# A new order of steps, more dummy products and items of 608 slots in a fused attention and two-layer expert kernel

## The chip, the cores and the metric

The kernel runs on one NeuronCore of one Trainium2 chip. The metric is the device time of one execution in microseconds (us). Five instruction streams work side by side: TensorE (PE, matrix products and transposes), VectorE (DVE), ScalarE (ACT), GpSimd (POOL) and SyncE (SP, which here only issues DMAs). Each runs its own list strictly in order and waits on the others by semaphores.

## The reference

```python
def _attn_ref(q, k, v, omega):              # (4, 8, 576, 64), 128 random features
    phi(x): h = x*scale @ omega.T - |x*scale|^2/2;  exp(h - max(h)) / sqrt(m)
    kv = phi(k).T @ v;  z = sum(phi(k))     # per batch and head
    return (phi(q) @ kv) / (phi(q) @ z + 1e-6)

def _moe_ref(x, w_in, w_out, g_ln):         # x: 2304 tokens x 512
    h = x @ w_in                            # 512 -> 1024
    solu = h * softmax(h)
    ln = (solu - mean) / sqrt(var + 1e-6) * g_ln
    return ln @ w_out                       # 1024 -> 512

def _moe2_ref(x, w_gate, w_output_gate, w1, w2):   # 8 experts, 512 -> 1024 -> 512
    e_idx = argmax(x @ w_gate);  gate_w = softmax(x @ w_gate)[e_idx]
    eom = sigmoid(x @ w_output_gate)
    for e in range(8):
        out[e_idx == e] = gate_w * eom[:, e] * (relu(x @ w1[e]) @ w2[e])
```

All is float32. With the inputs as drawn (seed 0) the eight experts get 561, 576, 0, 0, 0, 591, 576 and 0 of the 2304 tokens; four of them work.

## The kernel before

**The front.** The 2304 tokens are 18 tiles of 128. Every tile passes a chain of small steps, and each step is a function with a short name and the tile's number. `kp2` is the feature product of tile 2's keys on TensorE, `kx2` its maxima on VectorE, `ke2` its exponentials on ScalarE, `kv2` and `kw2` its part of the sums over the keys; `qp`, `qx`, `qe` are the same for queries, `qta`/`qtb` transposes of them, `qca`/`qcb` their copies, `na`/`nb`/`nc` the products with the sums, `ya`/`yb`/`yc` the divisions on VectorE, `xt` the transpose of the tile of x, `xh` and `xl` its upper and lower half. All large float32 products are made as three products of such halves (`mm3`): upper by upper, upper by lower, lower by upper. `ha`/`hb` are the two halves of h, `hxa`/`hxb`, `he`, `ma`, `mz`, `mb`, `mc`, `md`, `me` the softmax and the normalisation, `ta`/`tb` transposes, `u`/`l` the halves of the second product, `ua`, `ub`, `la` what takes them out of PSUM, `lo` the store. `ra` to `rh` work out the place of each token in its expert's list for six sets of tiles, and `zl` to `wc` load and split the first expert's weights and gather its first 256 tokens.

The weights of the first layer come as 16 chunks of eight-byte words. VectorE turns a chunk into float32 in five passes (`db`, `dc`, `dd`, `de`, `df`, L263 to L284), with one addition on POOL (`dp`) and a last pass for the lower half (`dl`). `ga` to `gd` fold the gate into the second weight.

`ORDER` is a table, written out by hand or by a planner, of all these steps. The helper `in_order` chains every instruction to the one before it on its engine, so that each engine runs its instructions in just this order. `LOADS` is the order of the loads on the SP queue; `pump` issues the next load as soon as the ring of buffers for its kind has one that the list has already used up. Work buffers are few: `big` has four PSUM half-banks (a feature product takes two), `sm` two.

**Dummy products.** A step `wuN` (`warm`) issues N products of a constant tile of ones with itself, 128x128, into columns of the PSUM bank of the key sums that nobody reads. A float32 product shows as two records in the trace.

**The experts.** Tokens are handled in items of `CAP` slots of one expert; `NSURE` is the number of items that is always run, `ceil(2304 / CAP)`, here 4, and more follow only if the experts' counts need more. `up` makes the hidden layer of an item for its slots (8 blocks of 128 features, 12 products each) in two runs of columns, `down` the output in blocks of 128 slots (`NBLK` = 5 blocks, 24 products each), scatters each block by an indirect DMA, and between the blocks the next item's tokens are transposed (`xpose`). The first item is split: its first 256 slots (`CA * P`) are run first, while the places of the last tiles are still being worked out (`rest`).

```python
    in_order(begin, 0)
    for what in ORDER:
        ...
        name = what.rstrip("0123456789")
        in_order(steps[name], int(what[len(name):]))
```

Of the kernel before, what the change touches and what calls it, by code (L numbers as in the profile page):

```python
# [67 lines left out]
ORDER = """
    da0 wu9 kp2 kx2 ke2 db0 da4 dc0 dd0 wu10 kp0 de0 df0 dp0 dh0 kx0 db4 dc4 dd4 de4 df4 wu4 kp1 ke0 dl0 dp4 kx1 da3
    wu10 kp3 db3 ke1 kv0 dc3 dd3 de3 df3 da6 wu2 kv1 kx3 dp3 dh4 da2 db6 dc6 dl4 dd6 de6 wu6 kp4 db2 dc2 dh3 dd2 da5  # L70
    de2 df2 ke3 df6 dl3 dp6 kx4 dh6 da1 wu12 kv2 dp2 dl6 kv3 ke4 db5 dh2 dc5 dd5 qp1 de5 df5 kv4 da8 dl2 qx1 dp5 da9
# [2 lines left out]
    qtb0 qcb1 kp7 da11 nb1 kx7 yb1 wu3 xt1 dp7 qcb0 dp9 ke7 dl8 qp2 db11 dc11 dd11 kv6 xh1 da10 dg9 qx2 de11 kp8 dh9
    df11 db10 qe2 na0 dc10 dl9 kv7 xl1 ya0 kx8 ga1 qta2 gb1 nb0 qca2 dp11 dg11 dd10 de10 ke8 df10 gc1 yb0 dp10 na2 gd1
    dg10 ya2 xt0 da12 ga3 dh11 qtb2 db12 dc12 kv8 gb3 dd12 qcb2 dl11 dh10 de12 dh7 nb2 xh0 df12 dl7 dp12 ga2 vc1 xl0
    qp4 gb2 yb2 da13 ha0 qx4 dg12 dh12 db13 qe4 dc13 dd13 de13 xt2 hb0 df13 dp13 xh2 hxa0 da15 xl2 dg13 dh13 qp3 hxb0
    gc2 he0 qx3 gc3 gd2 ma0 qe3 gd3 ga5 mz0 db15 ga4 mb0 gb5 dc15 qta3 gb4 qtb3 gc5 qca3 dd15 qcb3 ta0 mc0 gd5 de15
    na3 dl10 ca0 nb3 ya3 da14 sa0 tb0 kp9 db14 cb0 yb3 dc14 ha1 sb0 dd14 kx9 de14 ke9 hb1 df14 hxa1 dp14 df15 dg14
    qta4 hxb1 qtb4 dp15 dh14 gc4 he1 dl14 kv9 dg15 gd4 qca4 ma1 qcb4 na4 dh15 mz1 xt3 dl15 mb1 ga7 ya4 xh3 ga6 gb7  # L80
    kp10 xl3 gb6 mc1 ta1 kx10 gc6 ca1 ha2 md1 dl13 ke10 sa1 gd6 dl12 qp5 hxa2 hb2 qx5 qe5 nb4 hxb2 nc4 yb4 he2 kv10
    md0 yc4 me0 ma2 xt4 gc7 xh4 mz2 qta5 xl4 mb2 qtb5 qca5 gd7 tb1 qcb5 qp6 cb1 mc2 na5 sb1 qx6 u0 md2 qe6 ha4 ub0
    qta6 hxa4 qtb6 qca6 ya5 hb4 qcb6 na6 hxb4 ua0 nb6 he4 ya6 u1 ma4 mz4 mb4 ta2 kp12 ca2 yb6 mc4 sa2 me1 ta4 l0 ub1
    kx12 ua1 ca4 sa4 ke12 tb4 l1 la0 cb4 lo0 sb4 tb2 kp11 cb2 sb2 nb5 kx11 yb5 me2 ha3 ke11 md4 hb3 hxa3 la1 lo1 xt5
    hxb3 u2 xh5 he3 xl5 ma3 qp7 ua2 mz3 l2 ub2 mb3 qx7 mc3 qe7 md3 ta3 tb3 xt6 kv11 ca3 cb3 sa3 xh6 kp13 sb3 la2 xl6
    qta7 lo2 kx13 qtb7 qca7 me3 kv12 qcb7 ke13 na7 zc0 nb7 ya7 kv13 yb7 qp8 vc2 ha5 qx8 qe8 hb5 hxa5 u3 hxb5 he5 ma5
    ha6 mz5 ub3 ra0 mb5 hb6 hxa6 ta5 hxb6 tb5 ca5 u4 he6 me4 sa5 cb5 ua3 sb5 l4 ma6 ua4 ub4 qta8 la4 qtb8 qca8 lo4
    kp14 qcb8 na8 kx14 nb8 ya8 ke14 qp9 yb8 xt8 qx9 xt7 kw13 xh8 xh7 xl8 xl7 ha8 hb8 hxa8 u5 hxb8 qe9 mz6 he8 mb6 mc5
    ma8 ta6 tb6 ca6 l3 mz8 mc6 md5 sa6 mb8 cb6 md6 me5 sb6 me6 ub5 qta9 la3 ta8 tb8 ca8 lo3 kv14 qca9 qp10 ua5 na9 sa8
    mc8 qx10 cb8 qtb9 l5 md8 ya9 qe10 sb8 rc0 qcb9 kp15 la5 kp16 kx15 u6 kx16 ke15 ke16 l6 ub6 ua6 qp11 la6 kp17 qx11  # L90
    kv15 kx17 qe11 nb9 kv16 yb9 ke17 xt9 qta10 qta11 xh9 qca10 xl9 me8 lo5 qtb10 ha7 rd0 qcb10 qca11 na10 hxa7 nb10
    ya10 hb7 yb10 xt10 hxb7 qtb11 xh10 na11 he7 xl10 ha9 ya11 qcb11 ma7 mz7 hb9 mb7 hxa9 mc7 md7 me7 lo6 ta7 hxb9 tb7
    ca7 kv17 cb7 sa7 he9 sb7 nb11 ma9 u7 vc3 yb11 mz9 qp12 ua7 ub7 ra1 rc1 qp13 qx12 l7 qx13 qe12 rb0 qe13 ha10 re0
    rf0 rg1 la7 rg0 lo7 qta13 qtb13 hxa10 qca13 mb9 hb10 qcb13 mc9 md9 me9 u8 hxb10 he10 ma10 rb1 ua8 na13 ub8 ta9
    ya13 nb13 ca9 mz10 qta12 yb13 mb10 xt11 qca12 tb9 sa9 xh11 l8 mc10 xl11 cb9 md10 sb9 ha11 la8 hb11 hxa11 u9 hxb11
    he11 ma11 ta10 ua9 tb10 ca10 na12 ub9 mz11 cb10 mb11 rd1 rh0 sb10 rh1 qtb12 ya12 nc13 qcb12 rg3 ta11 nb12 yc13
    ca11 sa10 xt13 yb12 qp15 xh13 sa11 xt12 xl13 qp16 qx15 xh12 xl12 lo8 u10 qe15 qx16 qe16 l10 tb11 qta15 qtb15 me10
    re1 ub10 mc11 ua10 md11 la10 qca15 l9 qcb15 cb11 sb11 qp14 la9 lo9 u11 qx14 me11 lo10 qe14 na15 ub11 ra2 ua11
# [5 lines left out]
    tb14 ca13 sa14 cb14 ha16 sa13 ub12 xt17 tb13 xh17 rg11 sb14 rg10 rh10 rh11 cb13 hxa16 xl17 la12 sb13 hb16 lo12
    md14 me14 ha17 hxb16 he16 ma16 u13 mz16 mb16 mc16 hb17 ub13 hxa17 ua13 u14 hxb17 he17 md16 me16 ma17 l14 ua14 ub14
    mz17 ra3 mb17 rb3 mc17 ta17 rc3 tb17 ta15 rd3 re3 ca17 rf3 cb17 rg13 zl0 wa0 l13 rg12 mc15 sa17 rg14 rh12 la14
    rh13 ta16 la13 md15 md17 lo14 sb17 me17 wa1 rh14 lo13 zb0 ca16 tb16 u17 cb16 sa16 wa2 sb16 ca15 zg0 sa15 u16 wa3
    ub17 wb1 wc0 ua17 tb15 ua16 ub16 zt0 cb15 l17 me15 zh0 sb15 zs0 zg1 u15 wb2 wc3 la17 lo17 l15 ub15 ra4 ua15 rc4
# [1040 lines left out]
```

## Time and profile before

| | us |
|---|---|
| median of 3 timed runs | 661.83 (661.37 to 673.13) |
| the profiled execution | 665.99 |
| its span, first to last instruction | 664.3 |
| TensorE busy in the span | 639.2 (96%) |
| VectorE busy | 358.8 (54%) |
| ScalarE busy | 296.7 (45%) |
| POOL busy | 163.8 (25%) |
| mean granted TensorE clock | 0.983 of full |

Read it thus. TensorE is the engine that is nearly always busy, but three things are in its 96% that are not the reference's work: the dummy products, products at half the clock, and the modelled ends of pipelined products. What counts is therefore the spacing of its instructions, from the start of one to the start of the next, and not the length of a record. The front ends, and the experts begin, at about 417 us of the span.

### The profile page before, as it was taken

The numbers are of one execution on the slowest core, as the hardware profiler recorded it, in microseconds if no ns is written. First come the engines' busy times: TensorE is split into PE (matmuls) and PEld (weight loads), VectorE is DVE, ScalarE is ACT, GpSimd is POOL, SyncE is SP. The second block draws the span as 40 slices with busy tenths as digits, with TensorE's granted clock in tenths as the row PEclk, the third lists the DMA queues.
The fourth block names the chain that finished last, engine by engine and source line by source line (L and its number), as shares of the span: only waits on it lengthen the run. The fifth ranks groups of instructions, "written<-read, shape, count | busy, mean of one in ns | idle before, by whom it ended". The sixth has DMA issues, their size and how long they took to land. (4 is left out here: it accounts for less than half of the span.)

```text
span 664.3 us, 11388 instructions
## 1 busy us (share of the span) xinstructions
PE 639.2 (96%) x4434; PEld 582.0 (88%) x4434; DVE 358.8 (54%) x1010; ACT 296.7 (45%) x719; POOL 163.8 (25%) x133
## 2 busy tenths in 40 slices
...
GB/s 293 303 156 96 143 2 64 1 67 79 65 33 1 159 33 2 33 17 28 6 1 18 143 32 51 156 86 313 181 129 78 165 114 127 17 47 9 1 33 42
DMA packets 35199, 55.22 MB, mean 83 GB/s; under 512 B 2624, under 2 KB 21440, under 8 KB 35137
## 3 DMA queue, kind: packets, MB, share of 16 engines
...
q14 instruction: 26, 0.20, 0.1%
...
## 5 line engine op out<-in xcount | busy, mean ns | idle before, releaser
L155 PE MATMUL x<-w2h,lth 128*128 128x256 f32 (+1 forms) x288 | 83.8, 291 | 1.4 <-DVE xr L485 1.3
L155 PE MATMUL x<-w2l,lth 128*128 128x256 f32 (+1 forms) x288 | 81.9, 284 | 0.0
L155 PE MATMUL x<-w2h,ltl 128*128 128x256 f32 (+1 forms) x288 | 81.9, 284 | 0.0
L930 DVE SCALAR_TENSOR_TENSOR htl<-hp,hth 128x320 fp32r<-128x320 f32 (+2 forms) x64 | 31.4, 491 | 87.3 <-ACT hth L929 76.8
L558 POOL TENSOR_SCALAR s<-s,st 128x1024 f32<-128x1024 f32 x18 | 23.3, 1294 | 201.9 <-DVE st L554 93.4
L155 PE MATMUL hp<-xth,w1h 128*128 128x320 f32 (+1 forms) x224 | 70.3, 314 | 0.9 <-DVE htl L930 0.9
L155 PE MATMUL hp<-xtl,w1h 128*128 128x320 f32 (+1 forms) x224 | 70.2, 313 | 0.0
L155 PE MATMUL hp<-xth,w1l 128*128 128x320 f32 (+1 forms) x224 | 70.1, 313 | 0.0
L155 PE MATMUL yp<-w2h,hth 128*128 128x512 f32 x160 | 64.2, 401 | 0.0
L155 PE MATMUL yp<-w2l,hth 128*128 128x512 f32 x160 | 63.2, 395 | 0.0
L155 PE MATMUL yp<-w2h,htl 128*128 128x512 f32 x160 | 63.0, 393 | 0.0
L929 ACT ACTIVATE hth<-hp 128x320 fp32r<-128x320 f32 (+2 forms) x64 | 28.1, 439 | 74.4 <-PE hp L155 74.2
L155 PE MATMUL h<-w1h,xth 128*128 128x512 f32 x144 | 58.9, 409 | 0.0
L155 PE MATMUL h<-w1l,xth 128*128 128x512 f32 x144 | 56.9, 395 | 0.0
L155 PE MATMUL h<-w1h,xtl 128*128 128x512 f32 x144 | 56.9, 395 | 0.0
L155 PEld LDWEIGHTS x<-w2h,lth 128*128 128x128 f32 x288 | 54.1, 188 | 2.9 <-issue 1.5
L155 PEld LDWEIGHTS x<-w2l,lth 128*128 128x128 f32 x288 | 54.2, 188 | 0.3
L155 PEld LDWEIGHTS x<-w2h,ltl 128*128 128x128 f32 x288 | 54.3, 189 | 0.0
L525 DVE TENSOR_REDUCE st<-h 128x1 f32<-128x512 f32 x36 | 24.8, 689 | 45.2 <-PE h L155 45.2
L143 DVE TENSOR_TENSOR xtl<-xT,xth 128x512 fp32r<-128x512 f32 x36 | 24.7, 687 | 40.7 <-ACT xth L835 38.2
L372 ACT ACTIVATE qe<-qps,qmx 128x128 f32<-128x128 f32 x144 | 39.0, 392 | 17.1 <-DVE qmx L365 17.1
L951 ACT ACTIVATE y<-yp,scs 128x512 f32<-128x512 f32 x20 | 13.8, 690 | 69.3 <-PE yp L155 61.0
...
## 6 DMA issues: line engine op xcount, KB each, us to landing
...
```

What stands on the lines that cost most here:

```text
L143: return eng.tensor_tensor(out=out_, in0=a, in1=hi.bitcast(F32), op=ALU.subtract)
L155: return in_turn(nc.tensor.matmul(ps, **kw))
L372: nc.scalar.activation(out=e3[:, 2 * c + j, :], in_=pss[j][:, c, :], func=AF.Exp, bias=nmx[:, j, c:c + 1])
L525: nc.vector.tensor_reduce(out=st[:, n:n + 1], in_=of[f"h{n}", t], axis=AX.X, op=ALU.max, negate=True)
L558: nc.gpsimd.tensor_scalar(out=s, in0=s, scalar1=st[:, 10:11], scalar2=st[:, 11:12], op0=ALU.mult, op1=ALU.add)
L929: act = nc.scalar.activation(out=hi, in_=ps[:, 0:n], func=AF.Relu)
L930: dve = nc.vector.scalar_tensor_tensor(out=lo, in0=ps[:, 0:n], scalar=0.0, in1=hi.bitcast(F32), op0=ALU.max, op1=ALU.subtract)
L951: nc.scalar.activation(out=y, in_=ps, func=AF.Copy, scale=scs[:, col:col + 1])
```

## The change

Items have 608 slots instead of 640. The number of blocks stays 5, and the last block of an item has 96 slots: its gather, its transposes, its products in `down` and its scatter work on 96 rows. In `up` the two runs of columns of an item are 304 and 304 instead of 320 and 320, and in the first item 256 and 352 instead of 256 and 384. `NSURE` stays 4 (2304 / 608 = 3.8) and `NITEM` 11. Since a place within an expert's list no longer splits into item and slot by powers of two, `re` has three more small VectorE operations for each of the six sets: place is counted in units of `SHORT` = 32, and one is added for each item that lies before it. `LOADS` and `ORDER` are new tables with the same steps, but for the dummies: 14 groups with 83 products instead of 10 groups with 64. `warm` may now open the sums of a later batch, too.

```diff
-CAP = 640
-NBLK = CAP // P
+CAP = 608
+NBLK = -(-CAP // P)
+SHORT = NBLK * P - CAP
+def slots(j):
+    return min(P, CAP - j * P)
 LOADS = [(x[0], int(x[1:])) for x in """
-    k2 w0 w3 k0 w4 k1 w2 k3 v1 v0 v3 w6 c1 k5 w8 k4 w5 w9 c0 v2 w1 k6 v4 q1 q0 v5 k8 w7 k7 q4 k10 w11 q2 v7 v6 k11 v8
+    k0 w1 k3 w2 v0 k2 k4 k1 w3 w5 v1 w0 c1 q1 c0 k5 w9 w7 k6 w6 k7 w8 q2 q0 v2 w4 v3 v4 v6 q4 v7 k8 v5 k9 v8 w13 w11
 ...
 ORDER = """
-    da0 wu9 kp2 kx2 ke2 db0 da4 dc0 dd0 wu10 kp0 de0 df0 dp0 dh0 kx0 db4 dc4 dd4 de4 df4 wu4 kp1 ke0 dl0 dp4 kx1 da3
+    da1 wu9 kp0 wu4 kp3 kx0 db1 dc1 dd1 kx3 de1 ke0 df1 dp1 da2 wu8 kp2 ke3 kx2 wu5 kp1 dh1 db2 dc2 ke2 dl1 dd2 de2
 ...
-            if 0 not in kv_ps:
-                open_sums(0)
+            if not kv_ps:
+                open_sums(len(opened))
 ...
-            V.tensor_scalar(out=place, in0=place, scalar1=-1.0, scalar2=None, op0=ALU.add)
+            V.tensor_scalar(out=place, in0=place, scalar1=-1.0, scalar2=1.0 / SHORT, op0=ALU.add, op1=ALU.mult)
+            for k in range(1, NSURE):
+                V.scalar_tensor_tensor(out=place, in0=place, scalar=float(k * (CAP // SHORT + 1) - 1), in1=place,
+                                       op0=ALU.is_ge, op1=ALU.add)
             pli = r("pli", [P, n], I32)
-            V.tensor_copy(out=pli, in_=place)
+            V.tensor_scalar(out=pli, in0=place, scalar1=float(SHORT), scalar2=None, op0=ALU.mult)
 ...
         def xpose(x, xt, blocks, name):
             for j in blocks:
+                k = slots(j)
...
-                    transpose(ps[:, c, :], x[:, j, c * P:(c + 1) * P])
+                    transpose(ps[:, c, :], x[0:k, j, c * P:(c + 1) * P])
 ...
     def down(i, ht, blocks, between={}):
         for j in blocks:
+            k = slots(j)
...
-                mm3(ps, ht[0][:, f, j * P:(j + 1) * P], ht[1][:, f, j * P:(j + 1) * P],
+                mm3(ps, ht[0][:, f, j * P:j * P + k], ht[1][:, f, j * P:j * P + k],
```

Two places show how the new table moves instructions. The first is on TensorE, where the key sums of the second batch are opened (`kv1`, its dummies are the products with `ones`; `woT` are `ga`, `qT` are `qta` and `qtb`, `wog` is `gc`, `num` is `na`). Before:

```order
L155 MATMUL kv1_0_496<-ones_62 128x128 x5
L158 MATMUL woT0_567<-ident_61,f8_437 128x128 x4
L158 MATMUL qT1_0_574<-ident_61,qe1_457 128x128 x4
L155 MATMUL kv1_0_496<-v5_398,ke5_519 128x65 x4
L155 MATMUL kv1_1_497<-v5_398,ke5_519 128x65 x4
L155 MATMUL wog0_608<-glw_96,ft0_589 128x16 x4
L155 MATMUL num1_0_614<-kv_98,qt1_591 128x65 x4
L158 MATMUL qT0_0_624<-ident_61,qe0_506 128x128 x4
```

The same place on TensorE now:

```order
L162 MATMUL kv1_0_583<-ones_62 128x128 x12
L162 MATMUL kv1_0_583<-v5_593,ke5_413 128x65 x4
L162 MATMUL kv1_1_584<-v5_593,ke5_413 128x65 x4
L162 MATMUL kv1_0_583<-v6_442,ke6_564 128x65 x4
L162 MATMUL kv1_1_584<-v6_442,ke6_564 128x65 x4
L162 MATMUL kv1_0_583<-ones_62 128x128 x2
L166 MATMUL woT1_631<-ident_61,f9_542 128x128 x4
L166 MATMUL qT0_0_637<-ident_61,qe0_574 128x128 x4
L166 MATMUL qT1_0_647<-ident_61,qe1_504 128x128 x4
L162 MATMUL wog1_652<-glw_96,ft1_644 128x16 x4
```

Twelve dummies and two tiles' sums now stand in a row ahead of the first transposes, where five dummies and one tile's sums stood between them.

The second is on VectorE at the end of the front, before the experts' first products, which read `xtel` and `w1l`. `ea`/`er` are `rg`, `tsc` and `gw` are the last operations of `rf`, `lg` is `ub`, `ltl` is `sa`/`sb`. Before:

```order
L757 TENSOR_TENSOR gw_15_4794<-gw_15_4794,eo_15_4754 128x2
L759 CAST gwh_15_4801<-gw_15_4794 128x2
L760 COPY tsc_99<-gwh_15_4801 128x2
L761 TENSOR_TENSOR tsc_99<-gw_15_4794,gwh_15_4801 128x2
L768 TENSOR_SCALAR ea15_4805<-nums_97,flo_15_4790 128x128
L770 SCALAR_TENSOR_TENSOR er15_4807<-nums_97,col_15_4788,tsc_99 128x480
L143 TENSOR_TENSOR xtel_4483<-xTe_1_4811,xteh_4482 128x4x128
L768 TENSOR_SCALAR ea16_4855<-nums_97,flo_15_4790 128x128
L770 SCALAR_TENSOR_TENSOR er16_4857<-nums_97,col_15_4788,tsc_99 128x480
L973 COPY got_4874<-tab_2941 128x480
```

The same place on VectorE now:

```order
L781 TENSOR_SCALAR ea15_4800<-nums_97,flo_15_4716 128x128
L783 SCALAR_TENSOR_TENSOR er15_4802<-nums_97,col_15_4714,tsc_99 128x480
L150 TENSOR_TENSOR xtel_4547<-xTe_0_4769,xteh_4546 128x4x128
L150 TENSOR_TENSOR ltl17_4659<-lT17_1_4720,lth17_4658 128x512
L150 TENSOR_TENSOR w1l_72<-raw1_4543,w1h_71 128x1024
L150 TENSOR_TENSOR xtel_4547<-xTe_1_4808,xteh_4546 128x4x128
L781 TENSOR_SCALAR ea16_4822<-nums_97,flo_15_4716 128x128
L783 SCALAR_TENSOR_TENSOR er16_4824<-nums_97,col_15_4714,tsc_99 128x480
L150 TENSOR_TENSOR w1l_72<-raw1_4543,w1h_71 128x1024
L629 TENSOR_SCALAR lg_64<-x2_17_1_4827,st17_4468 128x16
```

The small operations of the last sets (`ra5`, `rf`) that stood between the two parts of `xtel` are now ahead of both or behind both, and both `w1l` passes stand in this place, one on each side of the second part. On TensorE the second transpose of the gathered tokens (`zt1`) had one product step behind it before the experts' first product, `l16`; now it has two, `u17` and `l17`.

## Rows read from the trace of the kernel before

**Rows 1.** The page: TensorE's share, and its granted clock in 40 slices.

```profile
PE 639.2 (96%) x4434; PEld 582.0 (88%) x4434; DVE 358.8 (54%) x1010; ACT 296.7 (45%) x719; POOL 163.8 (25%) x133
...

```

**Rows 2.** Windows: stretch, then each engine's busy us, clock, DMA share, GB/s.

```profile
20.00:40.00 20.00, 18.18 (x173) 17.37 (x172) 18.97 (x36) 13.89 (x44) 7.82 (x6) 0.93 0.76 230
...
60.00:80.00 20.00, 18.28 (x150) 16.41 (x149) 17.93 (x41) 12.30 (x32) 10.70 (x7) 1.00 0.39 123
80.00:100.00 20.00, 19.15 (x100) 17.48 (x100) 14.49 (x38) 11.23 (x30) 4.22 (x4) 0.66 0.14 51
```

**Rows 3.** Timeline of VectorE: start us, length, operation, count, idle before.

```profile
7.01 1.29 DVE L365 TENSOR_REDUCE kmx<-kps 128x4 f32<-128x512 f32 x2 [3.57 <-PE kps L155]
8.21 0.42 DVE L263 TENSOR_SCALAR f<-f 128x512 f32<-128x512 f32 x1
...
10.81 1.28 DVE L365 TENSOR_REDUCE kmx<-kps 128x4 f32<-128x512 f32 x2
...
71.37 0.68 DVE L143 TENSOR_TENSOR xtl<-xT,xth 128x512 fp32r<-128x512 f32 x1
```

**Rows 4.** Timeline of TensorE at the first and at a later product of h.

```profile
72.12 0.50 PE L155 MATMUL h<-w1h,xth 128*128 128x512 f32 x1
...
108.47 0.48 PE L155 MATMUL h<-w1h,xth 128*128 128x512 f32 x1
```

**Rows 5.** Timeline of TensorE at its start: dummies and the first feature products.

```profile
1.17 4.21 PE L155 MATMUL kv<-ones 128*128 128x128 f32 x18 [1.17 <-DVE mhalf L189]
5.31 1.66 PE L155 MATMUL kps<-bdr,kr 64*128 64x128 f32 x16
6.90 2.50 PE L155 MATMUL kv<-ones 128*128 128x128 f32 x20
9.33 1.16 PE L155 MATMUL kps<-bdr,kr 64*128 64x128 f32 x16
```

**Rows 6.** Windows of TensorE: stretch, busy us and count, granted clock, DMA share, GB/s.

```profile
36.00:38.00 2.00, 2.00 (x22) 0.78 0.03 9
...
42.00:44.00 2.00, 2.00 (x18) 0.52 0.81 284
...
80.00:82.00 2.00, 1.39 (x13) 0.87 0.99 354
...
94.00:96.00 2.00, 2.00 (x11) 0.72 0.01 4
```

**Rows 7.** Timeline of TensorE: instructions that waited, with the idle time in brackets.

```profile
34.73 0.48 PE L155 MATMUL kps<-bdr,kr 64*128 64x128 f32 x2 [1.27 <-ACT qe L372]
...
65.64 1.08 PE L155 MATMUL num<-kv,qt 128*128 128x65 f32 x8 [1.72 <-DVE w2h L331]
...
119.57 0.33 PE L158 MATMUL xT<-ident,xr 128*128 128x128 f32 x1 [0.80 <-DVE xr L485]
...
419.86 0.39 PE L155 MATMUL hp<-xtel,w1h 128*128 128x256 f32 x1 [2.32 <-DVE xtel L143]
```

**Rows 8.** Timeline of TensorE in the experts: where runs of one shape begin and end.

```profile
447.58 0.34 PE L155 MATMUL hp<-xth,w1h 128*128 128x384 f32 x1
...
451.98 0.34 PE L155 MATMUL hp<-xtl,w1h 128*128 128x384 f32 x1
...
480.07 0.39 PE L155 MATMUL yp<-w2h,hth 128*128 128x512 f32 x1
...
482.85 0.31 PE L155 MATMUL hp<-xth,w1h 128*128 128x320 f32 x1
...
487.98 0.31 PE L155 MATMUL hp<-xth,w1l 128*128 128x320 f32 x1
...
541.74 0.31 PE L155 MATMUL hp<-xth,w1h 128*128 128x320 f32 x1
```

**Rows 9.** Timeline of SP: the load of the first expert's w1.

```profile
373.25 1.01 SPq L812 DMA_DIRECT2D raw<-in_w  x2
```

More of the change, by code (lines that the diff above doesn't have):

```diff
@@ L74 @@
[L74 to L98, printed above, removed]
@@ L104 @@
[L104 to L108, printed above, removed]
@@ L109 @@
-    rd4 rb4 ra5 re4 rf4 rg15 la15 lo15 zt1 zm0 l16 zh1 zs1 rg16 la16 lo16
+    da1 wu9 kp0 wu4 kp3 kx0 db1 dc1 dd1 kx3 de1 ke0 df1 dp1 da2 wu8 kp2 ke3 kx2 wu5 kp1 dh1 db2 dc2 ke2 dl1 dd2 de2
+    wu7 kp4 df2 dp2 da3 kx1 da0 kx4 dh2 kv0 ke1 db3 wu7 kv1 dc3 dl2 db0 dc0 kp5 da5 db5 dd0 de0 dd3 da7 df0 ke4 db7
+    dp0 kx5 de3 dh0 df3 dc5 dp3 dd5 dh3 dl3 wu11 kp7 ke5 de5 wu11 kv2 df5 dc7 da6 dl0 kx7 qp1 da4 kv3 dp5 dd7 ke7 de7
+    df7 kv4 qx1 dp7 dh5 qe1 db6 qp0 dc6 dl5 dd6 dh7 kp6 de6 vc0 df6 da9 dl7 dp6 kx6 db9 dh6 dc9 dl6 dd9 de9 da8 df9
@@ new lines @@
+    db8 dp9 qx0 dg9 ke6 db4 qe0 kw4 wu12 kv5 kv6 wu2 ga1 dc4 qta0 dd4 de4 gb1 df4 qta1 gc1 qca0 dc8 dh9 dd8 qca1 qp2
+    de8 df8 na0 dp8 da13 qx2 kv7 dg8 dh8 ga0 qe2 dp4 qtb0 qcb0 gd1 db13 na1 dc13 dd13 wu1 qtb1 ya1 gb0 wu1 qp4 de13
+    qcb1 dh4 df13 ya0 dp13 kp8 qx4 gc0 dg13 kx8 qe4 nb0 dl4 yb0 da11 wu3 ga5 gd0 ke8 qta4 dl9 xt0 db11 nb1 dc11 dd11
+    da10 qp3 de11 gb5 df11 qca4 qtb4 db10 dp11 xh0 qta2 qx3 dh13 kv8 qca2 xl0 qcb4 dg11 qe3 dc10 na2 dd10 de10 dh11
+    df10 qtb2 yb1 qta3 dp10 qcb2 qtb3 qca3 xt1 ya2 qcb3 ga3 dg10 gb3 ga2 dl11 dh10 gc3 dl8 xh1 dl13 kp9 da15 gd3 xl1
@@ new lines @@
+    ha0 da12 kx9 db12 ke9 dc12 dd12 gc5 de12 nb2 df12 gb2 gd5 dp12 hxa0 gc2 vc1 yb2 hb0 dg12 db15 dh12 gd2 dc15 dd15
+    de15 ga4 na4 hxb0 gb4 nb4 df15 he0 ya4 dp15 ha1 ma0 mz0 nc4 yb4 dg15 hb1 dh15 hxa1 da14 yc4 qp5 hxb1 xt4 he1 qx5
+    xt2 kv9 xh4 ma1 qe5 mz1 mb0 kp10 xl4 xh2 kp11 kx10 mb1 na3 xl2 ke10 kx11 nb3 ya3 ke11 wu2 ta1 yb3 tb1 kv10 ca1 cb1
+    sa1 xt3 ta0 sb1 xh3 tb0 db14 ca0 ha2 xl3 cb0 mc1 sa0 sb0 md1 dl10 me1 dl15 hb2 hxa2 zc0 ha3 dc14 hxb2 dd14 he2
+    de14 df14 hb3 ma2 hxa3 mz2 ha4 mb2 hxb3 hb4 hxa4 mc0 he3 mc2 ma3 md0 mz3 qta5 md2 mb3 qtb5 qca5 gc4 qcb5 me2 hxb4
@@ new lines @@
+    he4 na5 gd4 dp14 kv11 ya5 mc3 dg14 ma4 nb5 ga6 yb5 ga7 gb6 ta2 gb7 xt5 ca2 tb2 xh5 gc6 sa2 xl5 ta3 tb3 ca3 ha5 cb3
+    sa3 dh14 sb3 cb2 dl14 gd6 sb2 gc7 hxa5 hb5 dl12 gd7 u2 me0 mz4 mb4 hxb5 mc4 he5 md4 me4 u1 ma5 ua2 mz5 ub2 l2 ua1
+    ub1 qp6 la2 lo2 kp12 qx6 l1 kx12 qe6 ke12 ta4 tb4 u0 ca4 cb4 sa4 sb4 qta6 ua0 ub0 qtb6 qp7 qx7 mb5 mc5 la1 kv12
+    qca6 qcb6 lo1 qe7 l0 qta7 na6 qca7 ta5 ya6 la0 lo0 tb5 ca5 nb6 md3 cb5 me3 sa5 kp13 sb5 yb6 kp15 kx13 xt6 kx15 u3
+    ke13 ke15 kv13 ub3 ra0 ua3 xh6 kp14 xl6 qp8 kx14 l3 qx8 ke14 qe8 na7 qtb7 ya7 ha6 la3 qcb7 nb7 hxa6 hb6 vc2 yb7
@@ new lines @@
+    u8 ke17 mb9 ta9 ua8 ub8 tb9 ca9 qp12 cb9 sa9 mc9 sb9 u7 qx12 md9 qe12 me9 l7 ub7 ra1 ua7 qta12 qtb12 qca12 qta11
+    qcb12 qtb11 qca11 kv17 qcb11 na11 ha10 ya11 la7 lo7 nb11 hxa10 hb10 vc3 yb11 xt11 hxb10 na12 xh11 he10 xl11 qp13
+    ya12 nb12 ma10 l8 qx13 yb12 qe13 mz10 xt12 rb0 mb10 rb1 re0 la8 qta13 xh12 lo8 qtb13 qca13 ta10 qcb13 tb10 ca10
+    na13 mc10 rf0 cb10 rg0 ha11 rg2 hb11 sb10 hxa11 xl12 sa10 rh0 ya13 ha12 hxb11 rg1 he11 rh1 hb12 hxa12 ma11 mz11 u9
+    mb11 hxb12 he12 ma12 ta11 ua9 tb11 ca11 mz12 ub9 mb12 rh2 qp15 mc11 sa11 l9 cb11 rc1 mc12 sb11 qx15 u11 la9 md12
@@ new lines @@
+    me12 qe15 lo9 rd1 qta15 qtb15 md10 re1 qca15 ta12 qcb15 tb12 me10 ca12 nb13 cb12 md11 me11 ub11 ua11 yb13 qp16
+    nc13 sb12 l11 yc13 qx16 u10 sa12 la11 qe16 lo11 qta16 ua10 ub10 ra2 l10 qca16 xt13 la10 rf1 rc2 qp14 xh13 lo10 rg3
+    rd2 na15 xl13 qx14 ha13 ya15 qe14 hb13 hxa13 qta14 hxb13 u12 qca14 he13 na14 ua12 ub12 nb15 ya14 qtb16 yb15 l12
+    qcb16 xt15 la12 xh15 ma13 mz13 rg5 mb13 qtb14 lo12 qp17 qcb14 xl15 mc13 ta13 qx17 tb13 nb14 ca13 md13 cb13 sa13
+    me13 na16 qe17 yb14 rb2 ya16 nb16 re2 xt14 qta17 xh14 ha15 qca17 xl14 yb16 rf2 xt16 na17 xh16 hxa15 ha14 xl16 ya17
@@ new lines @@
+    sb13 za0 hb14 hxa14 hb15 hxb14 he14 ma14 u13 mz14 hxb15 mb14 he15 rh3 l13 ub13 rg4 ma15 mz15 ta14 tb14 ca14 ha16
+    cb14 sa14 qtb17 hxa16 mb15 ua13 la13 mc15 qcb17 rh4 rh5 sb14 hb16 mc14 rg6 rg7 md14 me14 nb17 hxb16 rh6 he16 u14
+    yb17 rg8 ma16 mz16 xt17 ua14 ta15 ub14 xh17 ra3 tb15 ca15 l14 cb15 rc3 mb16 sa15 rd3 sb15 xl17 rb3 ta16 rh7 rh8
+    mc16 md15 re3 ca16 ha17 md16 rg9 rg11 hb17 me15 hxa17 rh9 la14 me16 sa16 rf3 tb16 rg10 cb16 hxb17 rh10 rh11 sb16
+    he17 rg14 lo13 u15 rg12 ma17 u16 mz17 ua15 rg13 mb17 ub15 rh12 rh13 ub16 ta17 mc17 lo14 ra4 rh14 rb4 zl0 ca17 zb0
```

42 lines of the change are left out of this document (21 added, 21 removed).

## The prediction

> **What bounds the kernel now.** The page comes first: TensorE is busy 96% of the span, and its granted clock stands below full in two stretches of the first 100 us [rows 1]. So the time is the sum of TensorE's own spacings, plus what it waits, plus dummies, plus half-rate stretches; another engine counts only where TensorE waits for it. I add up TensorE's steps by their spacing at full clock: the steps of the front come to 373 us without the dummies, and the experts begin at 417. The front thus holds about 44.6 us that is no work of the reference: 64 dummies of 0.243 us (ten take 6.90 to 9.33 [rows 5]), which is 15.6 us, and 29 us of waiting and slow clock.
>
> The windows say who is waited for: from 20 to 80 us VectorE is busy 18 to 19 us of each 20, afterwards less [rows 2]. I add up VectorE in the same way: 1.20 us for the two maxima of a tile (7.01 to 8.21) and 2.60 for the five passes of a weight chunk (8.21 to 10.81) [rows 3]; one pass over 128x512 is 0.6, a division 0.79. In the old list 63.3 us of VectorE's work stands up to `xl0`, which the first product of h needs. VectorE has its first maximum only at 7.01 and idles 8.7 us in all, so `xl0` ends at 72.0, and the product starts at 72.12 [rows 3, 4]. TensorE had done 44.1 us of work by then: the 28 us in between are VectorE's lead, whatever they were filled with. The same sum for `ma0`, nine steps later, asks for 29.0.
>
> After that the clock decides. It falls to the 1.2 GHz level twice: at about 37.1 us, after the 1.27 us wait, until 43.9, and at about 81.5 until 95.1, through a run of transposes and 16-column gate products (the shares 0.78, 0.52, 0.87 and 0.72 of two-us windows give these points); in between it stays at 2.4 GHz in spite of a wait of 1.72 us [rows 6, 7]. The first fall costs 3.4 us and lies in time that VectorE sets anyway. The second costs up to 13.6 / 2 = 6.8 us, and nothing covers it: at 108.47, with 72.9 us of work done, TensorE is 35.6 behind instead of 29 [rows 4]. From there to the experts nine waits add 9.0 us, the first 0.80, the last 2.32, all for VectorE [rows 7].
>
> **The change, part by part.** *608 slots.* Spacing of products by columns: 512 take (482.85 - 480.07) / 12 = 0.2317 us, 320 take (487.98 - 482.85) / 35 = 0.1466, 384 take (451.98 - 447.58) / 25 = 0.1760 [rows 8]. That is 0.45 ns a column. Items 1 to 3 have 2 x 8 x 12 = 192 products each whose columns go from 320 to 304: 576 x 16 x 0.45 ns = 4.1 us. Item 0 has 96 that go from 384 to 352: 1.4 us. The transposes of four short blocks lose 32 columns each in 16 transposes: 0.2 us. In `down` the short block keeps 512 moving columns and has 96 instead of 128 stationary ones, which no row shows; the spacing follows the moving columns through all three sizes above, all with 128 stationary columns, so I take 0. Lower bound: no loss is possible from less data; upper bound of the gain: 96 products a quarter shorter, 5.6 us. Sum 5.7, range 5 to 11, and nearer 5.7. It is on the path, for TensorE is spaced without gaps there.
>
> The Trainium skill, page "TensorE: Matmul & The Clock Gate", section "LDWEIGHTS (loading the stationary operand)", says that a weight load takes the number of stationary columns divided by 1.2 ns. If loads paced these products, 96 for 128 columns would give 96 x 27 ns = 2.6 us more by that rule, an estimate; the rows above speak for pacing by moving columns.
>
> *Three more operations in `re`*, six times. The small operations around them take about 0.2 us; 18 of them are 3.6 us of VectorE, after the stretch where it bounds. For the last set they stand in front of the table of item 0's places, under item 0's first products; I count 0, and 0.6 us if that cover is gone.
>
> *Dummies.* 83 x 0.243 = 20.2 us, 4.6 more than before. What they do to the time depends on whether VectorE's lead pays for them. In the new list VectorE's sums ask for less: 60.0 us of it up to `xl0`, 63.1 up to `yb1` (27 us behind with the 8.7 of idle, when `xt1` stands at 45.2 of TensorE's work), and at most 90.1 + 8.7 - 71.5 = 27.3 at `nb3`, which waits for `xl2`. TensorE itself brings 81 dummies by then (19.7), the start at 1.17, and 2.45 us for the first 18 records and the first feature product at half rate [rows 5]: 23.3. So 4 us are left for waits and falls before they cost anything. I take one fall of the first kind (3.4) and dribbles of waits for VectorE and ScalarE (about 3): 29.6 behind at 72 us of work instead of 35.6, a gain of 6.0. Bounds: 8.3 (no fall, VectorE's bound alone) and 1 (a long fall again, 6.8, less the smaller lead).
>
> *The loads.* The new `LOADS` brings what the list asks first (k0, w1, k3, w2), and k0 is as long as k2 was; by bytes no load comes later than its step. I leave VectorE's first maximum at 7.0; a later one would cost one for one.
>
> *Later waits.* Their sum was 9.0. At the end of the front the last wait (2.32) was for the second part of `xtel` behind 45 small operations on VectorE; now it stands before them, and `u17` and `l17`, 6 us of TensorE, cover it. But VectorE has more to do there: from `ha17` on 27 us of it against 28 us of TensorE, where before it was 34 against 41. I find four short waits in a hand count: `rh10` for `rg10`, 1.5; `rb4` for `ra4`, 0.5; `zt0` for the gather, 0.9; `zt1` for `zs0`, 1.0. Together 3.9, against 4.8 in the same stretch before. The load of w1 (`zl0`) moves on the SP queue behind `lo14`; before it was issued at 373.25, 44 us ahead of its use [rows 9], now about 21 ahead, still before. The other 4.2 us of waits, of the middle, I put at 2.6. In all 6.5, a gain of 2.5, between 5 and -3.
>
> **Sum.** 5.7 + 6.0 + 2.5 = 14.2 us off the profiled execution's 665.99: 651.8. The median is 4.2 below that execution. If all executions that are not profiled are shorter by as much, the new median is 647.6; if they are shorter because a fall of the clock is missing there, part of my gain is already in them, and it is 652. I forecast 650.
>
> **The rivals.** *No fall, few waits (643).* The dummies hold the clock to 100 us, and the lead of VectorE alone is left: 8.3 + 5 + 5.7 = 19.0, so 647.0 profiled and 643 for the median. For it: the wait of 1.72 us at 64 us dropped no clock [rows 7]. Against it: transposes and gate products still stand in a row in the new list, with no dummy between (`qtb2` to `gc3`, six groups of four transposes).
>
> *The clock falls as before (657).* Dummies stand only up to the 37th us of work, but for two; the long fall came later, at 53. If such a run of transposes drops it again, only 1 of the 8.3 is left, and with 1 of the late waits and 5.7 from the slots it is 7.7: 658.3 profiled, 656 to 657 for the median. The new `wu12` also waits for the copy that frees the sums' bank, so it may stand in TensorE's way rather than fill a wait; that ends in the same place.
>
> *Slower: a fifth item (707).* Four items of 608 hold 2432 slots, but if any expert gets 609 to 640 tokens, its work splits into two items and the loop behind the fixed four runs once more. An item takes 541.74 - 482.85 = 58.9 us [rows 8], so 650 + 57 = 707. It decides at 608 tokens; the largest expert here has 591, which speaks against it.
>
> **How the numbers follow.** Forecast 650 (646 to 654): 0.48. No fall: 0.20. Clock falls as before: 0.28. Fifth item, or a new wait of more than 10 us: 0.04. The range 642 to 658 holds the first three but their tails. A measurement of this kernel tells about 2% from no change, 13.2 us, so faster means below 648.6: the no-fall case and four tenths of the forecast, 0.39; slower 0.02; the rest 0.59.
>
> **What would show it.** The products of up to 304 columns spaced 0.139 to 0.140 us, those of the short block 0.232. VectorE's first maximum at 7.0, and its idle time up to `xl2` near 9. TensorE about 30 us behind its own work instead of 36 where 72 us of it are done: `ha2`, with 76.3 us of work ahead of it now, starting near 106. The clock at half for at most 7 us between 10 and 100 us. Waits of 1 us or less at `rh10`, `zt0` and `zt1`, none at `xtel`. I am wrong if the experts' products do not shrink with the columns, if the front ends later than 410, or if a wait above 3 us stands where the tail of VectorE meets the first item.

## The result, and the profile after

The changed kernel takes 653.26 us (median of four runs, 652.69 to 655.41), and the ratio to the kernel before is 0.988, with a 95% interval of 0.984 to 0.9919: faster by 1.2%, clear of no change but less than the 2% at which two versions are called different here. The forecast was 650 with a range of 642 to 658. The runs of the kernel before lie in two groups, at 661 to 666 and at 670 to 678 us with a lower mean clock (0.98 to 0.99 and 0.96 to 0.97), while the ten of the changed kernel lie at 651 to 656; ratios are taken from undisturbed runs. The profiled execution of the changed kernel took 652.88, beside 665.99 before.

First the page of the kernel before, its row of the granted clock in 40 slices, which belongs to [rows 1]; then the two rows of the page after.

```profile
PEclk9979969999999999999999999999999999999999
```

```profile
PE 629.5 (97%) x4472; PEld 571.7 (88%) x4472; DVE 361.3 (55%) x1028; ACT 293.5 (45%) x719; POOL 161.1 (25%) x133
...
PEclk9999899999999999999999999999999999999998
```

TensorE is busy 9.7 us less, and of the two low stretches only one short one is left. The windows of TensorE after (stretch, busy us and count, granted clock, DMA share, GB/s) show where:

```profile
36.00:38.00 2.00, 2.00 (x27) 1.00 0.97 259
42.00:44.00 2.00, 2.00 (x20) 1.00 0.62 190
76.00:78.00 2.00, 2.00 (x21) 0.74 0.95 282
78.00:80.00 2.00, 2.00 (x7) 0.50 0.77 219
80.00:82.00 2.00, 2.00 (x10) 0.91 0.23 63
404.00:406.00 2.00, 0.69 (x3) 0.66 0.00 0
406.00:408.00 2.00, 2.00 (x10) 0.50 0.03 8
```

Where before the clock fell at 37 and at 81 [rows 6] it stays at 2.4 GHz at 37, is at the 1.2 GHz level from about 77.0 to 80.4, and again from about 404.6 to 408. The first fall comes 2 us behind the end of a wait, the second within a wait, as the timeline of TensorE after shows (start, length, instruction, count; the idle time before it in brackets):

```profile
38.77 1.16 PE L162 MATMUL kps<-bdr,kr 64*128 64x128 f32 x14 [0.55 <-ACT qe L380]
...
75.07 0.66 PE L166 MATMUL woT<-ident,f 128*128 128x128 f32 x4 [2.20 <-POOL f L307]
...
78.05 0.79 PE L162 MATMUL h<-w1h,xth 128*128 128x512 f32 x1
...
108.16 0.48 PE L162 MATMUL h<-w1h,xth 128*128 128x512 f32 x1
...
384.92 0.70 PE L162 MATMUL tab<-er,ea 128*128 128x480 f32 x2 [1.51 <-DVE er L783]
...
393.27 0.39 PE L162 MATMUL places<-cnt,nums 128*128 128x8 f32 x2 [0.49 <-DVE cnt L693]
...
398.01 0.63 PE L166 MATMUL xTe<-ident,xge 128*128 128x128 f32 x4 [0.80 <-DMA xge<-x2d,idxe]
...
405.31 1.11 PE L166 MATMUL xTe<-ident,xge 128*128 128x128 f32 x4 [3.83 <-DVE xtel L150]
412.91 0.28 PE L162 MATMUL hp<-xteh,w1h 128*128 128x256 f32 x1
...
643.28 0.40 PE L162 MATMUL yp<-w2h,htl 128*96 128x512 f32 x1
```

The experts start at 412.91 with no wait between their first products. Before, their first product stood alone at 417.26 and the second waited until 419.86 [rows 7]; the last product before is the second line here:

```profile
417.26 0.28 PE L155 MATMUL hp<-xteh,w1h 128*128 128x256 f32 x1
...
656.29 0.40 PE L155 MATMUL yp<-w2h,htl 128*128 128x512 f32 x1
```

Counted from the end of that wait, the experts last to the last product 230.4 us instead of 656.29 - 419.86 = 236.4. So the front, its last wait included, gave 7.0 and the experts 6.0. Three of the hand-counted waits are where and as long as forecast: `rh10` 1.51 (1.5), `rb4` 0.49 (0.5), `zt0` 0.80 (0.9). The fourth, `zt1`, is 3.83 instead of 1.0, the longest of all. Its releaser is VectorE's split of `xtel`, and VectorE's timeline there shows what came before it; GpSimd's timeline stands below.

```profile
398.30 2.35 DVE L766 TENSOR_SCALAR gw<-gw 128x2 f32<-128x2 f32 x1
400.68 0.17 DVE L767 RECIPROCAL gw<-gw 128x2 f32<-128x2 f32 x1
400.76 2.20 DVE L768 TENSOR_SCALAR eo<-eo 128x2 f32<-128x2 f32 x1
...
404.57 0.68 DVE L150 TENSOR_TENSOR xtel<-xTe,xteh 128x512 fp32r<-128x512 f32 x1
```

```profile
398.23 4.71 POOL L150 TENSOR_TENSOR w1l<-raw,w1h 128x1024 fp32r<-128x1024 f32 x2
```

Two operations on 128x2 numbers, of the kind that takes 0.17 us elsewhere, took 2.35 and 2.20, and the second ends at 402.96, where GpSimd's two splits of the expert's weights (`wc0`, `wc3`) end at 402.94. The RECIPROCAL between them took its usual 0.17. The trace of the kernel before holds such pairs too, with larger operations: five of VectorE's splits of 128x1024 begin beside one of GpSimd's and took 2.36 to 2.61 us, where the other ten took 1.21 to 1.23. The first of the five, on VectorE before, and the split of GpSimd beside it, which ends at 402.41:

```profile
401.14 2.36 DVE L143 TENSOR_TENSOR w1l<-raw,w1h 128x1024 fp32r<-128x1024 f32 x1
...
400.00 2.41 POOL L143 TENSOR_TENSOR w1l<-raw,w1h 128x1024 fp32r<-128x1024 f32 x1
```

The products of an item's up half, and those of its short block, on TensorE after:

```profile
473.76 0.39 PE L162 MATMUL yp<-w2h,htl 128*96 128x512 f32 x1
473.99 0.30 PE L162 MATMUL hp<-xth,w1h 128*128 128x304 f32 x1
...
478.89 0.30 PE L162 MATMUL hp<-xth,w1l 128*128 128x304 f32 x1
```

(478.89 - 473.99) / 35 = 0.140 us for 304 columns, and 0.23 for 96 stationary and 512 moving columns. [rows 8] had 0.1466 for 320 and 0.2317 for 128 stationary ones.

### The profile page after: what moved, and what is told of

Same layout as the page of the kernel before. It is cut to its first block, busy times and chain, and to the rows that moved or that the text cites. A ratio compares the mean times of both kernels' runs of the same rounds, so it can differ in the third digit from the quotient of the medians.

```text
span 651.2 us, 11484 instructions
## 1 busy us (share of the span) xinstructions
PE 629.5 (97%) x4472; PEld 571.7 (88%) x4472; DVE 361.3 (55%) x1028; ACT 293.5 (45%) x719; POOL 161.1 (25%) x133
## 4 chain that ended last, share of the span: by engine, by line
PE 72%; DVE 8%; issue 6%; DMA 3%; POOL 1%; ACT 1%; POOLq 0%; DVEq 0%
PE x L162 15%; PE hp L162 13%; PE h L162 13%; PE yp L162 12%; PE num L162 4%; PE kv L162 3%; PE qps L162 2%; PE xT L166 2%; PE qT L166 2%; DMA out_y<-y,idxs 2%; PE lT L166 2%; PE kps L162 1%; PE wog L162 1%; DVE er L783 1%; DMA xg<-x2d,idxg 1%
## 5 line engine op out<-in xcount | busy, mean ns | idle before, releaser
L162 PE MATMUL x<-w2h,lth 128*128 128x272 f32 (+1 forms) x288 | 84.3, 293 | 0.0
L162 PE MATMUL x<-w2l,lth 128*128 128x272 f32 (+1 forms) x288 | 82.3, 286 | 0.0
L162 PE MATMUL x<-w2h,ltl 128*128 128x272 f32 (+1 forms) x288 | 82.2, 285 | 0.0
L945 DVE SCALAR_TENSOR_TENSOR htl<-hp,hth 128x304 fp32r<-128x304 f32 (+2 forms) x64 | 30.4, 474 | 82.5 <-ACT hth L944 70.1
L162 PE MATMUL hp<-xth,w1h 128*128 128x304 f32 (+1 forms) x224 | 68.5, 306 | 0.7 <-DVE htl L945 0.7
L162 PE MATMUL hp<-xtl,w1h 128*128 128x304 f32 (+1 forms) x224 | 68.4, 305 | 0.0
L162 PE MATMUL hp<-xth,w1l 128*128 128x304 f32 (+1 forms) x224 | 67.9, 303 | 0.0
L162 PE MATMUL yp<-w2h,hth 128*128 128x512 f32 (+1 forms) x160 | 64.1, 401 | 0.0
L162 PE MATMUL yp<-w2h,htl 128*128 128x512 f32 (+1 forms) x160 | 63.4, 397 | 0.0
L162 PE MATMUL yp<-w2l,hth 128*128 128x512 f32 (+1 forms) x160 | 63.3, 396 | 0.0
```

What stands on the lines that cost most here:

```text
L162: return in_turn(nc.tensor.matmul(ps, **kw))
L945: dve = nc.vector.scalar_tensor_tensor(out=lo, in0=ps[:, 0:n], scalar=0.0, in1=hi.bitcast(F32), op0=ALU.max, op1=ALU.subtract)
```

## The experiments

Differences between kernels are taken from medians of six or twelve runs. Eight kernels ran on one chip; `best`, `best_rh`, `after_early` and `ga2_wu` on another, on which the shortest run of the kernel before is 661.2, against 661.6 and 662.1 in the two sets of runs on the first.

**The two halves of the change.** `slots_only` is the changed kernel with the old tables; `order_only` is the kernel before with the new tables and the new dummies.

```diff
 slots_only, against the changed kernel
-LOADS, ORDER of the changed kernel
+LOADS, ORDER of the kernel before
 order_only, against the changed kernel
-CAP = 608
+CAP = 640
...
```

> Items of 608 slots with the old list of steps and the old dummies. Theory (the parts add up, the slots are worth 5.7 us): 5.7 us under the kernel before, near 656 where that takes 661.6, and all of it behind the front; the experts' first product still starts near 417. Rival (weight loads pace the short block too, 2.6 us more): 8 to 9 us under, near 653, and then the new list brings nothing. Rival (the slots bring nothing by themselves): within 1 us of the kernel before.

> The new list of steps, loads and dummies with items of 640 slots. Theory: what is left of the change, 2.5 to 3 us under the kernel before in timed runs (near 659), though 7 us under the profiled execution of before in the front, because that execution was itself 4 us above its median. The wait of 3.8 us at the second part of the last block (zt1) is there too. Rival (the list is worth the full 7 us of the front): near 655. Rival (the list brings nothing in timed runs): within 1 us of before.

`slots_only`: ratio 0.9911 (0.9839 to 0.9983), which leaves room for 1 to 11 us, and so for the theory and for the first rival. Its profiled execution took 667.82, with clock falls that the profile of before does not show: one from 66.8 to 77.0, and short ones at 176 and 401. These are its windows at the start and the end of the long one, behind the 1.71 us wait at 65.14, a wait that dropped nothing in the profile of before [rows 7], and the second and the last product of its experts:

```profile
66.00:68.00 2.00, 2.00 (x15) 0.69 0.63 182
...
76.00:78.00 2.00, 2.00 (x9) 0.75 0.00 0
```

```profile
426.92 0.39 PE L162 MATMUL hp<-xtel,w1h 128*128 128x256 f32 x1 [2.89 <-DVE xtel L150]
...
657.82 0.40 PE L162 MATMUL yp<-w2h,htl 128*96 128x512 f32 x1
```

So its experts begin 7 us later than before, against the expectation that they start near 417 as before, and take 657.82 - 426.92 = 230.9 instead of 236.4: 5.5 us for the slots, the first theory. `order_only`: 658.06 us (654.72 to 659.44), ratio 0.9854 (0.9783 to 0.9925). Its wait at `zt1` is 3.14, its experts start at 413.63, and the changed kernel (`after2` below, 652.66) is about 5 us below it, as the slots ask. The new list gave more than the 2.5 to 3 us expected in timed runs, and between that and the rival's 7 the interval does not decide.

**The dummies.** `after_nowu` and `before_nowu` are the two kernels with no dummies; `after_early` keeps the first eight groups, 62 dummies, and leaves out the 21 from `wu12` on. Its expectation speaks of 16 us; in the trace after, the 62 run in the first 30.

```diff
-    da1 wu9 kp0 wu4 kp3 kx0 db1 ...
+    da1 kp0 kp3 kx0 db1 ...
```

> The changed kernel without its 83 dummy products; nothing of the reference's computation is left out. Theory (they hold the clock through the waits that VectorE sets, and cost nothing there): the fall between 36 and 44 us is back, more waits show at half clock, and the time is 2 to 8 us longer, 655 to 661. Rival (VectorE sets the time there whatever fills the waits): within 1 us of 653. Rival (the dummies stand in the way): 2 to 6 us shorter, 647 to 651.

> The kernel before without its 64 dummy products; nothing of the reference's computation is left out. Theory: its first fall of the clock lies in time that VectorE sets, so without dummies the loss is smaller than for the changed kernel, 0 to 4 us. Rival (dummies are worth the same in both): the same difference as for the changed kernel. Rival (they are in the way): faster than before.

> The changed kernel without the 21 dummies from wu12 on; the 62 of the first 16 us stay; nothing of the reference's computation is left out. Theory (the early dummies keep the clock through the first waits, the later ones hold it to 80 us): 1 to 4 us longer than the changed kernel, 654 to 657, by a fall between 36 and 70 us. Rival (the later dummies only stand in the way): 1 to 3 us shorter. Rival (the first 62 do it all): within 0.7 us.

Without dummies the changed kernel takes 663.65 us (661.97 to 667.23, ratio 0.9938, 0.9892 to 0.9984): 11.0 more than `after2`, the changed kernel on the same chip (below), and beyond the 2 to 8 expected. The kernel before takes 670.85 without its own, ratio 1.004 (0.9985 to 1.0094): 2.7 us more by the ratio, between -1 and 6, which agrees with the 0 to 4 expected, and some 7 more against its shorter runs near 663 alone; either is less than 11.0, so the rival of the same difference is out. With the early dummies alone the changed kernel takes 660.05 (654.76 to 664.48), more than the 654 to 657 expected: the 21 late ones, 21 x 0.243 = 5.1 us of TensorE, are worth some 7. The windows of `after_nowu` show what they prevent:

```profile
36.00:40.00 4.00, 4.00 (x19) 0.50 0.00 0
...
48.00:52.00 4.00, 1.38 (x10) 0.82 0.45 132
...
56.00:60.00 4.00, 4.00 (x21) 0.50 0.53 196
```

Two falls, from about 34 to 47 and 51 to 61, and the first product of h at 88.05 instead of 78.05. In `after_early` one fall, from about 42 to 66, begins where the first late group is missing (`wu12` runs at 41.58 in the trace after), and h starts at 87.56. VectorE's timeline of `after_early` shows what the slow stretch does to the engine that paces the front:

```profile
58.05 1.29 DVE L373 TENSOR_REDUCE qmx<-qps 128x4 f32<-128x512 f32 x2 [5.81 <-PE qps L162]
...
66.53 0.16 DVE L492 TENSOR_SCALAR rd<-num 128x4 f32<-128x4 f32 x1 [5.38 <-PE num L162]
```

VectorE, on which the front rests, now waits for TensorE: up to 89 us its waits come to 20.6 us in all (21.8 in `after_nowu`), and to 11.7 in the changed kernel. The rival that the dummies stand in the way is out.

**The wait at `zt1`.** `after2` is the changed kernel again, on the same chip as the next three. `tail_dve` gives GpSimd's two splits to VectorE, behind the last split of `xtel`; `tail_rf` leaves GpSimd alone and moves the small operations of `rf4` (and `rg15`, which needs them) behind that split.

```diff
 tail_dve
-    ... l16 rg15 zh0 zs0 wc0 sb17 zt1 wa3 wa2 la16 lo15 wb1 wc3 zh1 lo16 zs1 rg16 wb2 ...
+    ... l16 rg15 zh0 zs0 sb17 zt1 wa3 wa2 la16 lo15 wb1 zh1 lo16 zs1 wb0 wb3 rg16 wb2 ...
 tail_rf
-    ... ua16 rf4 zt0 cb17 l16 rg15 zh0 zs0 wc0 sb17 zt1 ... zs1 rg16 wb2 ...
+    ... ua16 zt0 cb17 l16 zh0 zs0 wc0 sb17 zt1 ... zs1 rf4 rg15 rg16 wb2 ...
```

> The changed kernel once more, unchanged, as the measure for the three beside it on the same chip: 652 to 655, in one group, as before.

> The changed kernel with the two splits of item 0's weights that GpSimd does in the tail (wc0, wc3) given to VectorE instead, behind the split of the last xtel (zs1). Theory (GpSimd's tensor_tensor holds up two of VectorE's 128x2 operations of rf4 for its whole length, 2.4 us each instead of 0.17): those two take 0.2 us, the split zs0 ends 4.4 us earlier, the wait at zt1 falls from 3.8 to about 1 or less, and the time by 3 to 4 us, to 649 to 650. Rival (the wait is VectorE's own load): nothing is gained, or 1 to 3 us lost by the 2.4 us more on VectorE.

> The changed kernel with rf4 and rg15 moved behind zs1 in the list; GpSimd keeps its two splits. Theory (a clash of the two engines on certain operations): the 2.35 and 2.20 us move with rf4 out of the way of zs0, or another operation of VectorE is held up in their place; the wait at zt1 falls to 1 us or less in the first case, 3 us gained; stays above 2 in the second. Rival (VectorE's load): 0.6 us gained, the work of rf4 and rg15 without the long pieces.

`after2` took 652.66 (651.5 to 655.46), `tail_dve` 648.29 (646.09 to 650.73), `tail_rf` 647.41 (646.53 to 649.47): 4.4 and 5.2 us less, and in both no wait of TensorE at `zt1` is left. The experts start at 408.36 and 407.49. VectorE in `tail_dve`, with GpSimd idle there:

```profile
398.79 0.17 DVE L766 TENSOR_SCALAR gw<-gw 128x2 f32<-128x2 f32 x1
399.00 0.17 DVE L767 RECIPROCAL gw<-gw 128x2 f32<-128x2 f32 x1
399.08 0.15 DVE L768 TENSOR_SCALAR eo<-eo 128x2 f32<-128x2 f32 x1
```

The same instructions on the same data take 0.17 and 0.15. VectorE had 2.4 us more to do in this kernel and TensorE still gained, which puts the rival (VectorE's load) out. In `tail_rf` VectorE and GpSimd read:

```profile
398.76 0.69 DVE L150 TENSOR_TENSOR xtel<-xTe,xteh 128x512 fp32r<-128x512 f32 x1 [1.03 <-ACT xteh L877]
...
399.97 1.29 DVE L150 TENSOR_TENSOR w1l<-raw,w1h 128x1024 fp32r<-128x1024 f32 x1
...
402.86 0.67 DVE L766 TENSOR_SCALAR gw<-gw 128x2 f32<-128x2 f32 x1
```

```profile
397.77 5.73 POOL L150 TENSOR_TENSOR w1l<-raw,w1h 128x1024 fp32r<-128x1024 f32 x2
```

Here the split of `xtel`, which reads one operand from PSUM, runs its usual 0.69 beside GpSimd; `L766` is held up once more, until 403.53, and GpSimd ends at 403.50; and GpSimd's pair takes 5.73 instead of 4.71, with VectorE's own split of weights, two operands in SBUF, in its midst. The gain of 5.2 is more than the expected 3; it is as much as the wait (3.8) and the cost of the fall at 405 (1.4), and neither is left in this trace. The two held operations are no chance of one execution: in all seven traces in which GpSimd's two splits run beside `rf4` (`after`, `after2`, `order_only`, `after_nowu`, `after_early`, `ga2_late`, `ga2_wu`) two operations on 128x2 numbers take 2.20 to 2.40 us, each until within 0.04 us of the end of a split. In `order_only` the second is not the TENSOR_SCALAR on `eo`, which falls between the two splits there and takes 0.15, but the TENSOR_TENSOR of `gw` and `eo`, with both operands in SBUF.

The Trainium skill, page "SBUF — State Buffer", section "Who interferes with whom", says that VectorE and GpSimd share a pair of ports, held for a whole instruction by whichever issues first while the other blocks fully; tensor_scalar can ask for the pair, and an operation with two SBUF operands does against a GpSimd operation that reads SBUF. The 2.35 and 2.20 us, the 0.17 of the reciprocal, the 0.69 of `xtel` and the 5.73 agree with it.

**The wait at 75 us, and two versions with both moves.** `ga2_late` moves the transposes that wait 2.20 us for GpSimd behind the first products of h; `ga2_wu` leaves them and puts nine dummies in front of them; `best` is `tail_rf` and `ga2_late` together; `best_rh` also moves `rh10` and `rh11` behind `u15`. The wait at 75 looks in part like the same matter, though no run tests it: it ends with an operation of GpSimd that took 2.50 us instead of the 1.57 of most others of its kind, beside three splits of VectorE (72.39 to 74.68) with both operands in SBUF. GpSimd in the changed kernel:

```profile
72.51 2.50 POOL L307 TENSOR_SCALAR f<-f,glw 128x512 f32<-128x512 f32 x1
```

```diff
 ga2_late
-    ... ga3 dg10 gb3 ga2 dl11 dh10 gc3 ... xl1 ha0 da12 ...
+    ... ga3 dg10 gb3 dl11 dh10 gc3 ... xl1 ha0 ga2 da12 ...
 ga2_wu
-    ... ga3 dg10 gb3 ga2 dl11 ...
+    ... ga3 dg10 gb3 wu9 ga2 dl11 ...
 best_rh
-    ... cb16 hxb17 rh10 rh11 sb16 he17 rg14 lo13 u15 rg12 ma17 ...
+    ... cb16 hxb17 sb16 he17 rg14 lo13 u15 rh10 rh11 rg12 ma17 ...
```

> The changed kernel with ga2, the transposes that wait 2.20 us for GpSimd at 75 us, moved behind the first products of block 0 (ha0). Theory (this wait and the clock's fall behind it are lost time, since VectorE is ahead there): h of block 0 starts at 75.7 to 76 instead of 78.05, no fall between 76 and 81, and the time is 2 to 3.5 us shorter, 649.5 to 651. Rival (VectorE is what bounds there, so that the wait only moves on to the next product): within 0.7 us of the changed kernel, with a wait of about 2 us for VectorE before 105 us.

> The changed kernel with 9 more dummies (2.2 us) in the wait of ga2; nothing of the reference's computation is changed. Theory (the wait is what drops the clock at 75 to 82 us): the wait shows as work, the fall is gone in nearly all runs, and the time is 1 to 2 us below the changed kernel's median. Rival (the transposes and short products around it drop the clock): no difference. Rival (the dummies run past the wait): up to 1 us longer.

> The changed kernel with both moves: rf4 and rg15 behind zs1, and ga2 behind ha0. Theory (the two lost times are separate): 5.2 us of the one and 1 to 2 of the other, so 645 to 647. Rival (VectorE's lead gives the front's gain back later): as with rf4 and rg15 alone, 647 to 648.

> The same, and rh10 and rh11, the one-hot products that wait 1.5 us for rg10 at 385 us, moved behind u15. Theory: those 1.5 us are TensorE's own loss, and the time is 1 to 1.5 us below the kernel with both moves, near 645. Rival (the wait comes back at zt0, zt1 or the first item, since VectorE sets the tail): no difference.

`ga2_late` took 651.62 (650.0 to 653.95), 1.0 below `after2` with overlapping runs, and `ga2_wu` 652.83 (651.64 to 653.67): neither difference shows. Yet in both traces the early fall is gone: h starts at 74.96 and at 76.58. The windows of `ga2_wu` tell where the time went:

```profile
76.00:78.00 2.00, 2.00 (x18) 1.00 1.05 277
...
188.00:190.00 2.00, 2.00 (x17) 0.89 0.40 117
190.00:192.00 2.00, 2.00 (x12) 0.50 1.00 323
192.00:194.00 2.00, 2.00 (x16) 0.75 0.35 99
```

A fall of some 3.4 us now stands at 189, where no engine makes TensorE wait: it begins towards the end of a run of 32 products of 65 columns. In the profile of the changed kernel the same 32 products run at full clock. First `ga2_wu`, then the changed kernel:

```profile
186.05 4.18 PE L162 MATMUL kv<-v,ke 64*128 64x65 f32 x32
```

```profile
188.54 3.92 PE L162 MATMUL kv<-v,ke 64*128 64x65 f32 x32
```

All five traces without the fall at 77 (`ga2_late`, `ga2_wu`, `best`, `best_rh`, and `tail_rf`, whose edit lies 320 us later) have it at 189; the traces of the changed kernel, `after2` and `tail_dve` have it at 73 to 82 and none at 189. Since `tail_rf` has no early fall either, the two edits at 75 us are not shown to be what took it away. The other kernels with the new list fit: `after_nowu`, with no fall where h begins, has one at 200.7, at the end of the same 32 products, and `order_only` and `after_early`, with a fall where h begins, have none there. In each of these traces the fall stands in one of the two places. Why the one run of products drops the clock in some executions and not in others stays open.

`best` took 647.13 (645.88 to 651.79), ratio 0.9731 (0.9615 to 0.9848), against 647.41 of `tail_rf` alone on the other chip: no difference that shows, as the rival says. `best_rh` took 647.91 (646.97 to 649.45), 0.8 above `best` with overlapping runs, no gain either: the wait of 1.51 for `er` comes back as 1.29 at 389.98, with 0.58 for GpSimd behind it. Versions with the small operations moved are thus the fastest found, at 647 us, some 2.6% below the kernel before (`tail_rf`: ratio 0.9737, 0.966 to 0.9814).

## Why the prediction was off in size

The kernel got faster, as forecast, and its time lies in the stated range; the gain was too large. From 661.83, the median then known, it was forecast as 11.8 and measured as 8.6. Of the 3.3 us between 650 and 653.26, 1.1 are in the sum for the profiled execution (14.2 forecast, 13.1 measured between 665.99 and 652.88), and 2.2 in the step from that execution to the median.

*608 slots: right.* 5.7 forecast, 5.5 in `slots_only` and 6.0 in the changed kernel. 304 columns take 0.140 as said, and 96 stationary columns 0.23, so the 2.6 us more by the Trainium skill's rule on weight loads are not there: in these runs the weight loads do not pace the products.

*Dummies and front: nearly right, by another path.* The clock stays up at 37 as hoped. One fall of 3.4 us is left; it costs half its length, 1.7, where I had put a cost of 3.4. The waits up to `ha2` come to 3.7 instead of about 3, and 2.2 of them are the wait for GpSimd at 75, which no sum of mine held, because I followed VectorE alone. Fall and waits together are thus less than forecast, 5.4 against 6.4, and yet `ha2` starts at 108.16 and not near 106, by my count of work 31.9 behind instead of 29.6, a gain of 3.7 and not 6.0: the count was short, for the steps ahead of `ha2` have spacings of 79.3 us in the trace and not 76.3 (75.0 before, where I had 72.9). The dummies carry this gain: without them 11.0 us are lost. VectorE's first maximum came at 6.50, not 7.0, and its waits up to `xl2` are 11.7, not near 9.

*Later waits: the step that failed.* "`zt1` for `zs0`, 1.0" was 3.83, and the fall of the clock within it cost about 1.4 more (2.7 us of products at half rate). The waits of the middle, put at 2.6, were 0.5; that error the other way, which is luck, hides the first in the sum. From 108 us to the experts the waits sum to 7.1 and not 6.5, against 9.0 before; with the fall, 0.5 of the 2.5 is left. I had counted VectorE's operations by their usual lengths and never asked what GpSimd does at the same time, though the trace of before held five operations of twice their length for it. `tail_rf` takes this wait and this fall away and gives 5.2 us, `tail_dve` 4.4.

*The sum.* By these terms 6.0 + 3.7 + 0.5 = 10.2 against 13.1 measured. The other 2.9 are in my counts of work: by the spacings in the two traces the steps ahead of `ha2` grew by 4.3 us and not by 3.4, and all steps of the front together shrank from 377.2 to 375.3, by about 0.5 each for `x`, `num` and three kinds of transposes; I had taken them as equal. Why they shrank is not shown.

*From the profiled execution to the median: the other step that failed.* I put the 4.2 us between them halfway, 651.8 to 650, 1.8 less; in the changed kernel the median is 0.4 more (652.88 and 653.26). Of the two cases named, 652, in which the 4.2 were a matter of the clock in that one execution, is the one that came out. With `zt1` as forecast and without its fall, 4.2 less, about 649 would have been measured, an estimate; `tail_rf`, with no wait there at all, measured 647.4.

Of the rivals, "no fall" did not come in the changed kernel; in the versions without the fall at 77 one of as much finds another place. "Clock falls as before" and "a fifth item" did not come either. Two of the marks of error named in the prediction were met: a wait above 3 us stood where VectorE's tail meets the first item, and the front ended at 412.91, later than 410. The second mark was too tight, for the forecast itself asks for 419.86 - 8.5 = 411.4; and the sign "1 us or less" for `rh10` contradicts the 1.5 of its own sum.
